# Block-sparse attention with a max-out feed-forward: global scores of two heads over two tiles at once, keys and queries loaded in row pairs and turned by halves on TensorE

## Chip, cores and metric

One core of one Trainium2 chip. The metric is the device time of one execution in microseconds; lower is better. Engines are named as in the profile: PE is TensorE's matmul stream, PEld its weight loads, DVE is VectorE, ACT is ScalarE, POOL is GpSimd, SP issues most DMAs.

## The reference

Four batches of eight heads, 768 positions of 64 numbers, in blocks of 32 (24 blocks). A query block sees its own block and the two beside it, three sampled blocks, and the first and the last block; the first and the last query block see everything. The result goes through three 512 x 768 matrices, of which the maximum is taken, and a 768 x 512 matrix.

```python
scores = scale * np.matmul(q, k.transpose(0, 1, 3, 2))
mask = np.abs(blk_i - blk_j) <= window
mask = mask | (blk_i == 0) | (blk_j == 0) | (blk_i == n_blocks - 1) | (blk_j == n_blocks - 1)
for qb in range(n_blocks):
    for kb in sampled_blocks[qb]:
        mask[qb * block:(qb + 1) * block, kb * block:(kb + 1) * block] = True
scores = np.where(mask, scores, -1000000000.0)
attn = softmax(scores)            # with 1e-09 added to the sum
x = (attn @ v), heads side by side
h = np.maximum(np.maximum(x @ w1, x @ w2), x @ w3)
return (h @ w_out).astype(np.float32)
```

All inputs are float32. The kernel splits each operand of the large matmuls into a high and a low float16 part and adds three products (`PASSES`: high-high, high-low, low-high).

## The kernel before

**Units.** A batch is twelve units of 64 queries with all eight heads: eleven sparse ones (two query blocks, 256 gathered keys for each) and one global unit "G" (the first and the last query block, all 768 keys). After every fourth unit the feed-forward for their 256 tokens is put on the list: 216 matmuls of 256 columns (L894, 18 groups of 12), then 36 of 512 columns (L920). The order of units in a batch is G, 10, 8, 9, then 0 to 3, then 4 to 7.

**Keys and queries.** `load_k` brings a batch's keys into three stage tiles, two DMAs for each (one for the even rows, one for the odd ones), so that a run in HBM is one row of one head, 256 bytes. Queries come the same way into `qn`, in pieces of up to 128 rows for twice 128 partitions. `turn_k` (L566) and `prep_q` (L643) turn them on PE: one turn is four transposes of 128 x 128 float32 into one PSUM bank, each for two heads side by side; ACT writes the scaled high part (L574, L647) and DVE the low part (L577, L650) into `kt` and `qt`. A batch has six turns of keys; each of the twelve query tiles (three in each batch) has two turns. Turns, and the transposes of a finished unit (L867), share one PSUM bank (`tp_ps`), and, while an operation's priority is below `Plan(4)`'s 4, the two banks of the second score tile as well.

**Attention.** `gather` copies sampled key blocks into `kg` (L685; a register that holds the block's number is loaded first, L351, on the engine that copies) and fetches rows of values from HBM with an indirect DMA on POOL (L699). `sparse_item` makes the scores of four heads (L775), the maximum (L749), the exponents (L784), and `probs` splits them (ACT L727, POOL L728) and turns them by a DMA transpose on SP (L732); for the first units (`TURNED`) PE turns them instead (L720). `values` multiplies by the values (L799). The global unit does four items, one for each `i` and `hd`: scores (L818) of two heads `u` at the same `hd`, over the two key tiles `a`, both in one score tile of two banks; maximum over both (L746), two exponents (L828), values (L840). `hd` picks partitions 0 to 63 or 64 to 127 of `qt` and `kt`, `u` the output rows 0 to 63 or 64 to 127. `finish_unit` divides (L858 to L860), turns (L867) and stores the high and low part for the feed-forward.

**Weights.** `prep_weights` loads 24 pieces (8 groups `g` of three), casts each (L437 on POOL or L440 on ACT, whichever the planner finds sooner free), puts it together on DVE (L444), scales it by a sum of squares on PE (L388, L376), and writes a high part (ACT L466) and a low part (DVE L475). The first feed-forward needs the first six groups, its second matrix the last two.

**The order.** `Plan` is a list of operations with an engine, an assumed duration, keys read and written, and a priority. `Plan.order` runs through them once at build time, and the instructions are emitted in that order, so every engine works through a fixed list. Where the plan sees PE without work for more than 0.2 us, `gaps` and `idle` fill the hole with matmuls whose result is never used (fillers, L991), one for each 0.11 us. A filler is a real instruction: it takes its time whether or not the hole is there.

## Time and profile before

| | |
|---|---|
| median of 3 runs | 678.12 us (677.71 to 678.25) |
| profiled execution | 669.58 us, its span 667.8 us |
| mean granted clock | 0.992 |
| busy DVE, ACT, POOL | 57%, 57%, 47% of the span |
| DMA | 110.45 MB, mean 165 GB/s; 162,993 of 199,065 packets under 512 bytes |

The profiled execution is faster than the median of the runs by 8.5 us; stages and durations are read from it, and differences are put on the median. A busy PE says little by itself here, since the fillers count as busy. The rows that matter are therefore shown by stage: from the start to the first scores, to the first feed-forward matmul, to the second feed-forward, and the rest.

### The profile page before, as it was taken

What the parts mean: (1) busy time and instruction counts of PE and PEld (TensorE: products, weight loads), DVE (VectorE), ACT (ScalarE), POOL (GpSimd) and SP (SyncE); (2) the same over time, 40 slices, a digit from 0 to 9 for tenths busy, and PEclk for the clock granted to TensorE, in tenths of its full rate; (3) what the DMA queues carried; (4) which work ended last, traced back from release to release, by engine and by line L of the source; (5) the groups of instructions that cost most, each with busy time, mean ns of one, the idle gap of its engine ahead of it and who ended that gap; (6) DMA issues with size and microseconds to landing.
All of it is one profiled execution on the core that took longest, in us unless ns stands there. A gap on an engine that the chain in (4) does not pass through costs nothing.

```text
span 667.8 us, 26558 instructions
## 1 busy us (share of the span) xinstructions
PE 626.4 (94%) x11249; PEld 482.8 (72%) x11249; DVE 382.4 (57%) x1076; ACT 379.8 (57%) x789; POOL 314.1 (47%) x405
## 2 busy tenths in 40 slices
PE   8797997999999998989999988999999989999997
PEld 7675876886886875777867865777868857758684
DVE  1598786886754666653754863355746765543120
ACT  0366664668745867766538764386548764463111
POOL 1333567353553667645235776255236775462010
PEclk9999999899999999999999999999999999999999
DMA  9599699999865889998486799989575897593000
GB/s 191 173 275 255 145 252 184 218 167 237 212 144 147 112 163 196 216 215 195 115 225 113 131 179 225 220 137 177 149 191 101 165 213 153 119 164 74 33 1 32
DMA packets 199065, 110.45 MB, mean 165 GB/s; under 512 B 162993, under 2 KB 184610, under 8 KB 198946
## 3 DMA queue, kind: packets, MB, share of 16 engines
q1 hardware_dynamic: 189090, 73.61, 57.7%
q0 software_dynamic: 9856, 35.15, 20.9%
q8 instruction: 88, 1.44, 0.9%
q14 instruction: 31, 0.25, 0.1%
HBM read 68.77 MB, written 12.70 MB: 122 GB/s over the span
## 4 chain that ended last, share of the span: by engine, by line
PE 83%; issue 4%; DMA 4%; DVE 4%; ACT 3%; another core or an unknown queue 0%; SPq 0%; DVEq 0%; POOL 0%; ACTq 0%; POOLq 0%
PE f_ps L894 42%; PE f_ps L920 13%; PE av_ps L799 6%; PE s_ps L775 6%; PE f_ps L991 5%; DMA pts<-phl 2%; PE s_ps L818 2%; PE tp_ps L867 2%; PE tp_ps L643 2%; PE av_ps L840 1%; PE tp_ps L566 1%; DMA vscr<-vhl 1%; PE tp_ps L376 1%; PE tp_ps L388 1%; DVE nm L749 1%
## 5 line engine op out<-in xcount | busy, mean ns | idle before, releaser
L894 PE MATMUL f_ps<-xg,w_hl 128*128 128x256 f16 x2592 | 304.4, 275 | 7.3 <-issue 4.2
L894 PEld LDWEIGHTS <-w_hl 128*128 128x128 f16 x2592 | 250.1, 99 | 49.4 <-issue 17.2
L728 POOL TENSOR_TENSOR phl<-pr,phl 128x512 f16<-128x512 f32 (+1 forms) x110 | 126.8, 1155 | 110.2 <-ACT phl L727 74.0
L902 DVE SCALAR_TENSOR_TENSOR hf<-f_ps,hf 128x256 f32<-128x256 f32 x144 | 60.8, 422 | 94.6 <-PE f_ps L894 86.3
L906 POOL TENSOR_TENSOR ht<-hf,ht 128x256 f16<-128x256 f32 x72 | 51.4, 714 | 124.0 <-ACT ht L905 123.9
L699 POOL DMA_INDIRECT vg<-vscr,rows_of x88 | 83.4, 948 | 48.8 <-PE av_ps L799 19.2
L784 ACT ACTIVATE pr<-s_ps,nm,qsm 128x256 f32<-128x256 f32 x176 | 92.5, 562 | 18.9 <-DVE nm L754 17.1
L920 PE MATMUL f_ps<-wo_hl,ht 128*128 128x512 f16 x432 | 99.7, 379 | 1.5 <-issue 1.5
L749 DVE TENSOR_REDUCE nm<-s_ps 128x2 f32<-128x512 f32 x88 | 60.4, 686 | 40.5 <-PE s_ps L775 28.4
L920 PEld LDWEIGHTS <-ht 128*128 128x128 f16 x432 | 40.5, 98 | 48.0 <-issue 5.7
L991 PE MATMUL f_ps<-ident 128*128 128x256 f16 x561 | 71.6, 277 | 1.5 <-DVE ident L268 1.5
L727 ACT CAST phl<-pr 128x512 f16<-128x512 f32 (+1 forms) x110 | 65.2, 594 | 2.2 <-DMA pts<-phl 0.3
L905 ACT CAST ht<-hf 128x256 f16<-128x256 f32 x72 | 29.0, 403 | 63.7 <-DVE hf L902 62.4
L991 PEld LDWEIGHTS <-ident 128*128 128x128 f16 x561 | 53.8, 100 | 10.4 <-issue 2.3
L799 PEld LDWEIGHTS <-pts 128*32 128x32 f16 x4224 | 39.5, 95 | 22.7 <-issue 19.6
L799 PE MATMUL av_ps<-vg,pts 128*32 128x65 f16 (+1 forms) x4224 | 47.4, 196 | 8.8 <-issue 6.2
L685 POOL COPY kg<-kt 128x256 f16 x88 | 37.6, 450 | 34.9 <-PE s_ps L775 29.7
L898 ACT ACTIVATE hf<-f_ps 128x256 f32<-128x256 f32 x72 | 27.5, 382 | 41.8 <-PE f_ps L894 39.0
L775 PE MATMUL s_ps<-kg,qt 64*32 64x256 f16 x2112 | 45.7, 272 | 5.8 <-issue 3.1
L685 ACT COPY kg<-kt 128x256 f16 x88 | 31.6, 402 | 26.1 <-PE s_ps L775 21.2
L775 PEld LDWEIGHTS <-qt 64*32 64x32 f16 x2112 | 24.1, 91 | 15.8 <-issue 12.3
L754 DVE TENSOR_SCALAR nm<-nm,qsm 128x1 f32<-128x1 f32 x192 | 32.5, 207 | 2.3
(150 smaller groups left out, 636.0 us busy)
## 6 DMA issues: line engine op xcount, KB each, us to landing
stage<-in_moe_w_dram SPq DMA_DIRECT2D x14, 511.0 KB
vscr<-vhl SPq DMA_DIRECT2D x12, 520.0 KB
stage<-in_k_dram SPq DMA_DIRECT2D x24, 256.0 KB
stage<-in_v_dram SPq DMA_DIRECT2D x12, 512.0 KB
qn<-in_q_dram SPq DMA_DIRECT2D x20, 256.0 KB
out_dram<-ob SPq DMA_DIRECT2D x20, 256.0 KB
stage<-in_moe_w_out_dram SPq DMA_DIRECT2D x5, 511.8 KB
vg<-vscr SPq DMA_DIRECT2D x16, 130.0 KB
```

Source lines behind the costliest of these rows:

```text
L685: (A.copy if by == 2 else eng.tensor_copy)(out=dst, in_=src)
L699: plan.add("POOL", 1.02, lambda c=c: L.indirect_dma_start(out=vgj[: 6 * HB, c].rearrange("p e h x -> p (e h x)"), out_offset=None, in_=vsc ...
L727: plan.add("ACT", 0.05 + 0.565 * n / 512, lambda: A.copy(out=hl[:, :n], in_=prt[:, :n]), r=PRK(it), w=[hk], pri=pri, alts=[("DVE", 0.6 * n ...
L728: plan.add("POOL", 1.2 * n / 512, lambda: L.tensor_tensor(out=hl[:, n : 2 * n], in0=prt[:, :n], in1=hl[:, :n], op=ALU.subtract), r=PRK(it) ...
L749: plan.add("DVE", 0.7, lambda: V.tensor_reduce(out=n[:, 0:2], in_=both()[:, :, :256], axis=AX.X, op=ALU.max), w=[ks, (ks, 0), (ks, 1)], pr ...
L775: T.matmul(out=s_ps[r * BS : (r + 1) * BS, hd * 512 : hd * 512 + 256], lhsT=q_t[hp, tq, 2 * i + u, q0 + c * BS : q0 + (c + 1) * BS], rhs=k ...
L784: plan.add("ACT", 0.56, lambda hd=hd: A.activation(out=prt[:, hd * 256 : hd * 256 + 256], in_=s_of(job)[:, hd * 512 : hd * 512 + 256], fun ...
L799: T.matmul(out=av_ps[r * BS : (r + 1) * BS, 2 * i + hd, :w], lhsT=pv[:, tp, hd, e, r * BS : (r + 1) * BS], rhs=vgj[:, c, e, h, (D + 2) * t ...
L894: T.matmul(out=pf, lhsT=w_hl[f][:, j, g, wp], rhs=x[:, g, xp, :], start=g == 0 and n == 0, stop=g == G - 1 and n == 2)
L902: plan.add("DVE", 0.42, lambda h=h, pf=pf: V.scalar_tensor_tensor(out=h, in0=pf, scalar=2.0 ** -14, in1=h, op0=ALU.mult, op1=ALU.max), r=[ ...
L920: T.matmul(out=f2_ps, lhsT=hts[:, f, hp, t * P : (t + 1) * P], rhs=wo_hl[f // 3][:, f % 3, wp], start=f == 0 and n == 0, stop=f == NF - 1 ...
L991: T.matmul(out=f_ps[fb][:, :256], lhsT=x[:, :P], rhs=x, start=True, stop=True)
```

## The change

Three things, and numbers of the plan.

1. **Loads.** Keys are loaded as values are (`load_v(k, ...)`): one DMA for a stage tile, a partition holding two neighbouring rows of each head, 512 bytes in one run. Queries come into `qn[P, H, 2, D]` the same way, one DMA for 256 rows, or two (224 and 32 rows) in the group that ends the sequence.
2. **Turns.** Since a head's 64 columns for one parity `e` are no longer beside the next head's, a turn is eight matmuls with the identity as the moving operand, each with 64 weight columns (one head), into the upper or lower half of the PSUM rows. They are plain float32 matmuls where there were transposes.
3. **Global scores.** `global_items` takes both `hd` for one `i`: for each key tile `a` a score tile whose two banks are the two heads `hd`, with `hd` as the innermost loop. Each of the two tiles has its own maximum (two columns); a third DVE operation joins them, then come two bias operations and the four exponents. Both score tiles are held until their exponents are done.

The numbers: `TURNED` 2 to 3 (unit 2 is turned on PE too), `POOL_LOW` with 2 in it (the low part of the third piece of each weight group is made by two POOL operations, L471 and L472, in place of one on DVE), all 24 casts of weights on POOL, sampled copies of slot 0 on ACT in place of DVE for the first units (with their register loads), `Plan(8)` for 4 (three turning banks for longer), `WSL` 0.5 for 0.8 (weights earlier), earlier loads of the next batch, and priorities.

```diff
-PV, TURNED, POOL_LOW = -1, 2, ()
-TP, HOLD, WPRI, WSL = 0.45, 3.0, 2.0, 0.8
+PV, TURNED, POOL_LOW = 0.2, 3, (2,)
+TP, HOLD, WPRI, WSL = 0.45, 3.0, 2.0, 0.5
...
-    qn = sbuf([P, 2, H, D], F32, "qn")
+    qn = sbuf([P, H, 2, D], F32, "qn")
...
-    plan = Plan(4)
+    plan = Plan(8)
...
-            ), 0)] if 1 else ())
+            ), 0)] if 0 else ())
...
-        sts = k_sts[b] = load_k(b, pri, after)
+        sts = k_sts[b] = load_v(k, b, pri, after)
...
-            src = stage[sts[a]].rearrange("p (e g x) -> p e g x", e=2, g=G)
+            src = stage[sts[a]].rearrange("p (h e d) -> p e h d", h=H, e=2)
...
                     for y in range(4):
                         g, e = 2 * half + y // 2, y % 2
-                        T.transpose(tv[:, y], src[:, e, g], ident)
+                        for hd in range(2):
+                            T.matmul(out=tv[hd * D : (hd + 1) * D, y], lhsT=src[:, e, 2 * g + hd], rhs=ident, start=True, stop=True)
...
-        for p0, w, r in pieces(n):
-            p0, e = p0 % P, p0 // P
-            plan.add("SP", 0.45, lambda p0=p0, e=e, w=w, r=r: Y.dma_start(out=qn[p0 : p0 + w, e], in_=src[r : r + w]),
-                     r=after, w=[("qn", e, p0 > 0)], pri=pri, land=2.2, move=1.8 * w / P)
+        for p0, w, r in [(0, whole, r0)] + ([(whole, 2 * P - whole, 0)] if whole < 2 * P else []):
+            plan.add("SP", 0.45, lambda p0=p0, w=w, r=r: Y.dma_start(
+                out=qn[p0 // 2 : (p0 + w) // 2].rearrange("p h e d -> p h (e d)"),
+                in_=q[b, :, r : r + w, :].rearrange("h (p e) d -> p h (e d)", e=2)),
+                r=after, w=[("qn", p0 > 0)], pri=pri, land=2.2, move=2.05 * w / 256)
...
-                for g in range(G):
-                    T.transpose(tv()[:, g], qn[:, e, 2 * g : 2 * g + 2], ident)
-            hi, lo = (to[:, t, :, e * P : (e + 1) * P] for t in range(2))
+                for h in range(H):
+                    T.matmul(out=tv()[h % 2 * D : (h % 2 + 1) * D, h // 2], lhsT=qn[:, h, e], rhs=ident, start=True, stop=True)
+            hi, lo = (to[:, t].rearrange("p g (x e) -> p g x e", e=2)[:, :, :, e] for t in range(2))
...
-                by = (0,1,2)[t] if pri < 8 else t
+                by = (2,1,2)[t] if pri < 8 else t
...
+    def global_items(U, b, i, q_c, pri):
...
+        for a, job in enumerate(jobs):
+            def scores(a=a, job=job):
+                for x, (tq, tk) in enumerate(PASSES):
                     for u in range(2):
+                        for hd in range(2):
+                            hp = slice(hd * 64, hd * 64 + 64)
+                            T.matmul(
+                                out=s_of(job)[u * 64 : u * 64 + 64, hd * 512 : hd * 512 + 384],
+                                lhsT=q_t[hp, tq, 2 * i + u, 192:256],
+                                rhs=kt[hp, :, tk, 2 * i + u, a],
+                                start=x == 0, stop=x == 2,
+                            )
...
+            plan.add("DVE", 0.95, lambda na=na, job=job: V.tensor_reduce(
+                out=na[:, 0:2], in_=s_of(job).rearrange("p (d x) -> p d x", d=2)[:, :, :384], axis=AX.X, op=ALU.max),
...
-        pri -= 0
+        pri -= 2
...
-        by = (0,1,2)[t] if 8 > 0 else t
+        by = (2,1,2)[t] if 8 > 0 else t
...
-        if x == max(gx, 6 if U < 12 else 6) and b + 1 < B:
-            prep_v(b + 1, U + 3, [("unit", U)])
-        if x == (6 if U < 12 else 4) and b + 1 < B:
+        if x == max(gx, 4 if U < 12 else 5) and b + 1 < B:
+            prep_v(b + 1, U + 7, [("unit", U)])
+        if x == (4 if U < 12 else 3) and b + 1 < B:
...
-            prep_q(nx // 12, nx % 12 // 4, nx - 2.0, [("unit", 0)] if U == 1 else ())
+            prep_q(nx // 12, nx % 12 // 4, nx - 3.0, [("unit", 0)] if U == 1 else ())
```

In the program fillers fall from 561 to 464. Before the first scores there are 153 and then 122, from there to the first feed-forward matmul 314 and then 322, after it 94 and then 20.

On PE, just after the sums of squares of the first keys (`stage_78` and `stage_79` are the first two key tiles, L566 and L643 turn keys and queries, L991 are fillers), before:

```order
L376 MATMUL tp_ps<-qsm_99,ones 128x1
L566 MATMUL s_ps_141<-ident,stage_78 128x8x16 x4
L566 MATMUL s_ps_141<-ident,stage_79 128x8x16 x4
L643 MATMUL tp_ps<-ident,qn 128x128 x4
L991 LDWEIGHTS ident
L991 MATMUL f_ps_143<-ident 128x256
```

and now, L556 and L635 being the turns, L1000 the fillers:

```order
L376 MATMUL tp_ps<-qsm_99,ones 128x1
L556 MATMUL s_ps_141<-ident,stage_78 64x8x16 x8
L556 MATMUL s_ps_141<-ident,stage_79 64x8x16 x8
L1000 LDWEIGHTS ident
L1000 MATMUL f_ps_143<-ident 128x256
L635 MATMUL tp_ps<-ident,qn 64x128 x8
```

A turn is now eight instructions with 64 output rows each. Between the first query turn and the second stand 36 fillers (there were 7), and ahead of each of the three sums of squares of keys 14 (there were 28).

On ACT, at the end of the register loads with which its list begins, before:

```order
L351 TENSOR_LOAD samp
L351 ISA x2
L574 ACTIVATE kt_89<-s_ps_141,ksm_103 128x8x64 x2
L647 ACTIVATE qt_97<-tp_ps,qsm_99 128x4x128
L647 ACTIVATE qt_97<-s_ps_141,qsm_99 128x4x128
L574 ACTIVATE kt_89<-s_ps_141,ksm_103 128x8x64
L574 ACTIVATE kt_89<-tp_ps,ksm_103 128x8x64
L440 CAST ob_134<-xg_128 128x512
```

and now:

```order
L351 TENSOR_LOAD samp
L351 ISA x2
L639 ACTIVATE qt_97<-tp_ps,qsm_99 128x512
L564 ACTIVATE kt_89<-s_ps_141,ksm_103 128x8x64 x2
L639 ACTIVATE qt_97<-tp_ps,qsm_99 128x512
L564 ACTIVATE kt_89<-s_ps_141,ksm_103 128x8x64 x2
L564 ACTIVATE kt_89<-tp_ps,ksm_103 128x8x64
L564 ACTIVATE kt_89<-s_ps_141,ksm_103 128x8x64
```

There are 28 such loads ahead of the first high part where there were 14, and the casts of weights are gone from between the high parts.

On POOL, in the stretch where the first weights are split (`kt_90` holds the weights on their way, `vg` the gathered values, `kg` the sampled keys), before:

```order
L685 ISA
L685 COPY kg_93<-kt_89 128x256
L728 TENSOR_TENSOR phl_117<-pr_113,phl_117 128x512
L437 CAST ob_134<-xg_129 128x512
L728 TENSOR_TENSOR phl_118<-pr_114,phl_118 128x512
L699 DMA vg_94<-vscr_136,rows_of 96x2080 x2
```

and now:

```order
L437 CAST ob_135<-stage_83 128x512
L471 TENSOR_SCALAR kt_90<-kt_90,w_s 128x512
L472 TENSOR_TENSOR w_hl_63<-kt_90,w_hl_63 128x4x128
L691 DMA vg_94<-vscr_136,rows_of 96x2080 x2
L437 CAST ob_134<-xg_129 128x512
L471 TENSOR_SCALAR kt_90<-kt_90,w_s 128x512
L472 TENSOR_TENSOR w_hl_64<-kt_90,w_hl_64 128x4x128
L677 ISA
L677 COPY kg_93<-kt_89 128x256
```

A gather (L691) and the copies of sampled keys now stand behind two-step low parts of weights, eight of which are on POOL altogether.

129 lines of the change are left out of this document (61 added, 68 removed).

## The prediction, made before the changed kernel had run

> **What bounds the kernel now.** I read the page's busy shares first, then four stages by windows, then the fillers in the same windows, then PE's timeline. The page's first line, and the four stages, with the busy time of PE, PEld, DVE, ACT and POOL in each, then the clock, and the share and rate of DMA:
>
> ```profile
> PE 626.4 (94%) x11249; PEld 482.8 (72%) x11249; DVE 382.4 (57%) x1076; ACT 379.8 (57%) x789; POOL 314.1 (47%) x405
> 0.00:34.78 34.78, 28.24 (x255) 23.83 (x255) 11.87 (x44) 9.15 (x14) 9.87 (x39) 1.00 0.80 187
> 34.78:100.60 65.82, 59.83 (x1141) 48.67 (x1141) 54.56 (x138) 44.71 (x87) 30.49 (x36) 1.00 0.90 231
> 100.60:164.87 64.27, 58.82 (x1068) 46.79 (x1067) 48.30 (x129) 40.66 (x83) 32.67 (x35) 0.95 1.04 204
> 164.87:663.20 498.33, 479.49 (x8790) 363.55 (x8789) 267.69 (x767) 284.61 (x608) 241.05 (x297) 1.00 0.76 151
> ```
>
> and the fillers alone (PE, PEld), for the same windows:
>
> ```profile
> 0.00:34.78 34.78, 20.73 (x153) 15.36 (x153) 1.00 0.80 187
> 34.78:100.60 65.82, 38.66 (x315) 29.52 (x314) 1.00 0.90 231
> 100.60:164.87 64.27, 11.04 (x88) 8.16 (x86) 0.95 1.04 204
> 164.87:663.20 498.33, 1.20 (x8) 0.78 (x8) 1.00 0.76 151
> ```
>
> Ninety-four per cent says little. In the last stage PE is busy 479.5 of 498.3 us with next to no fillers, and no other engine above 285: there every us of PE work counts in full. In the first two stages 59 us of PE are fillers; what decides are the chains over DMA, ACT and DVE which those fillers cover. The third, from the first feed-forward matmul to the second feed-forward, lies between.
>
> **Stage 1, the loads.** The rate of DMA in forty slices of 0.75 us of the first 30 us, PE's rows there, and one from POOL's and one from ACT's list:
>
> ```profile
> GB/s 0 0 7 133 287 229 202 203 218 218 218 218 216 218 218 213 212 313 325 284 254 53 45 42 130 340 349 307 335 358 207 53 14 0 0 82 266 373 386 322
> 6.10 0.39 PE L388 MATMUL tp_ps<-qn 128*128 128x128 bf16 x4 [0.59 <-DMA qn<-in_q_dram]
> 9.38 0.62 PE L388 MATMUL s_ps<-stage 128*128 128x128 bf16 x8
> 9.85 3.22 PE L991 MATMUL f_ps<-ident 128*128 128x256 f16 x28
> 36.25 5.41 PE L991 MATMUL f_ps<-ident 128*128 128x256 f16 x48
> 10.44 0.99 POOL L483 MEMSET ob<- 128x512 int32 x2 [7.73 <-issue]
> 20.54 1.26 ACT L574 ACTIVATE kt<-s_ps,ksm 128x512 f16<-128x512 f32 x2 [18.32 <-PE s_ps L566]
> ```
>
> Queries and keys (2 MB in 256-byte runs) flow at about 218 GB/s; the values behind them (512-byte runs) at about 313. In 512-byte runs the 2 MB take 2.0 / 313 = 6.4 us for 9.2. Forty-eight fillers take 5.41 and 28 take 3.22, so one is 0.11 us; 31 fewer are 3.4 us, and the first row shows a wait for queries that shorter loads cut. But ACT gets in the way: POOL's fourteen register loads took the 7.73 us of that gap (2.71 to 10.44), 0.55 us each, so ACT's 28 end near 2.7 + 15.4 = 18.1 us. Before, its first high part came at 20.54. So the stage gains at least 20.54 - 18.1 = 2.4 us, and, if PE also loses fewer waits (by its window it was not busy for 6.5 us of the stage), up to 5. I take 3.5, with dearer turns (below) in it.
>
> **The turns.** Two turns in the third stage and what follows each:
>
> ```profile
> 138.59 0.60 PE L643 MATMUL tp_ps<-ident,qn 128*128 128x128 f32 x4
> 139.03 1.15 PE L894 MATMUL f_ps<-xg,w_hl 128*128 128x256 f16 x9
> 17.42 0.73 PE L376 MATMUL s_ps<-ksm,ones 128*128 128x1 f32 x6
> 45.84 0.82 PE L840 MATMUL av_ps<-vhl,pts 128*64 128x65 f16 x36
> L840 PE MATMUL av_ps<-vhl,pts 128*64 128x65 f16 (+1 forms) x576 | 11.7, 196 | 0.8 <-issue 0.8
> ```
>
> A turn takes PE from 138.59 to 139.03, 0.44 us, 0.110 for each of four transposes. What a plain float32 matmul costs is seen in one place only: three instructions of the program (L376) stand as six records, so each is done in two. A new turn is therefore sixteen records of 128 moving columns. Their price is bounded. From below by bfloat16 records of 128 columns (L388, eight from 9.38 to 9.85, 0.059 each), two at a time in the two halves of the columns: 16 x 0.059 / 2 = 0.47 us. From above by float32 records like the transposes, one at a time: 16 x 0.110 = 1.76. For two at a time speaks L840, which also alternates 64-column halves: 36 in 0.82, of which one matmul's own 0.196 is tail, so 0.018 each, where 65 columns of L388's price would be 0.030. The nearest row in type and in columns is the transpose, the nearest in shape of tile L840; I take 0.110, halved: 0.88 us, or 0.44 more for each turn.
>
> The Trainium skill, FP8 and Floating Point Precision (TensorE Precision Notes), speaks against the change: true float32 goes through the array in four passes; the two records of L376 fit that if each makes two. By that rule alone, at one bfloat16 pass of 0.059 us, eight matmuls would take 1.89 us a turn, and the sum below would end near 719 us in place of 674. TensorEngine Tiling (Key Properties) says that different tiles load weights and multiply in parallel, which would halve it to 0.94 (677 us); L840's row agrees in kind, but no run here shows it for float32.
>
> How many turns count is in the same windows, for L566 and then L643 in the last stage, four records to a turn:
>
> ```profile
> 164.87:663.20 498.33, 10.85 (x72) 8.51 (x72) 1.00 0.76 151
> 164.87:663.20 498.33, 11.25 (x72) 8.19 (x72) 1.00 0.76 151
> ```
>
> Eighteen and eighteen; four more lie in stages 2 and 3, eight in stage 1. So +36 x 0.44 = 15.8 us in stage 4 and 0.9 each in stages 2 and 3.
>
> **The global scores.**
>
> ```profile
> 34.79 1.52 PE L818 MATMUL s_ps<-kt,qt 64*64 64x384 f16 x24
> 42.24 1.16 PE L818 MATMUL s_ps<-kt,qt 64*64 64x384 f16 x12
> 43.34 0.72 PE L991 MATMUL f_ps<-ident 128*128 128x256 f16 x5
> 60.32 0.85 PE L775 MATMUL s_ps<-kg,qt 64*32 64x256 f16 x48
> 61.10 0.72 PE L991 MATMUL f_ps<-ident 128*128 128x256 f16 x5
> ```
>
> Twelve matmuls of one head take 1.10 us (0.092 each), but where two heads stand one behind the other 24 take 1.46, from 34.79 to the fillers at 36.25 (0.061): their halves of the rows overlap where they meet. Alternating all along is what L775 does over eight tiles, 48 in 0.78; with 384 for 256 columns and four tiles for eight that is 0.049 each. I take 0.049 (bounds 0.061 and the 0.040 of perfect sharing): twelve groups of twelve in stage 4 save 12 x 12 x 0.043 = 6.2 us (4.5 to 7.5), the first batch 1.3. The maximum and its bias grow by one small DVE operation for each pair, beside feed-forward matmuls. The pair's two score tiles are now held together, so the next sparse scores wait until the last exponents; feed-forward matmuls lie behind them on PE and cover it at 1 to 2 us for each of three batches. I charge nothing. Nor for queries written to every second element, the earlier loads of the next batch and the priorities: DVE and ACT, which carry them, are busy 268 and 285 of stage 4's 498 us. Were a write of a query half to take twice its time there, PE would meet it only where a turn's bank is wanted at once.
>
> **Stages 2 and 3.** Eight more fillers in stage 2 (+0.9) against the 1.3 saved and 0.9 for turns: +0.5. In stage 3, PE waits in these rows:
>
> ```profile
> 113.47 0.56 PE L799 MATMUL av_ps<-vg,pts 128*32 128x65 f16 x48 [2.54 <-DMA pts<-phl]
> 147.15 3.65 PE L991 MATMUL f_ps<-ident 128*128 128x256 f16 x32
> 151.50 0.85 PE L775 MATMUL s_ps<-kg,qt 64*32 64x256 f16 x48 [0.69 <-ACT wo_hl L466]
> ```
>
> The 32 fillers and the wait behind them cover the last weights, which `WSL` 0.5 brings earlier; 74 fewer fillers after the first feed-forward matmul are 8.1 us. Of 3.2 us of waits in these rows and of the clock of 0.95 over 64 us (another 3.2) I count half as gone, 3.2. With 0.9 for turns stage 3 gives -10.4. What the plan's earlier weights lean on is POOL:
>
> ```profile
> L728 POOL TENSOR_TENSOR phl<-pr,phl 128x512 f16<-128x512 f32 x15 | 21.1, 1407 | 27.5 <-ACT phl L727 18.8 <-issue 5.4 <-DMA qn<-in_q_dram 3.2
> L437 POOL CAST ob<-stage 128x512 f16<-128x512 bf16 x7 | 6.5, 951 | 1.6 <-DVE kt L444 1.6
> ```
>
> (from 34.78 to 164.87 us). Thirteen more casts (24, where POOL had 11) at 0.95 are 12.4, and eight low parts at two operations of L728's 1.41 are 22.5. POOL goes from 63.2 of 130.1 us to 98: three quarters full, in a fixed order, with gathers behind. DVE and ACT are relieved of the same operations.
>
> **The sum.** -3.5 + 0.5 - 10.4 + (15.8 - 6.2) = -3.8 us against the span of 667.8 us, which would become 664.0. Put on the median of 678.1: 674.3 us.
>
> **The rivals.**
>
> *Halves that do not overlap.* If the float32 halves go one at a time, a turn is 1.76 us: 40 turns at 0.88 more, 35.2, and 3.5 in stage 1 give 678.1 - 3.8 + 38.7 = 713.0 us, slower. The place is PE in stage 4. Without the 17.6 us for 40 turns the sum is -21.4, so the change loses from a turn of 0.44 + 21.4 / 40 = 0.98 us on. For it: every float32 record in the trace is a full-width one. Against: L840.
>
> *Cheap turns.* If a record costs no more than a bfloat16 one and halves overlap, a turn stays near 0.47: -3.8 - 16.4 - 1.6 (stage 1) = -21.8 gives 656.3 us. For it: nothing in the trace shows what 128 moving columns cost in such a record. Against: the transposes, of the same type, take 0.110.
>
> *POOL late.* The low parts stand ahead of gathers, so values wait, or the first feed-forward waits for weights. Eight at 2.8 us are 22.5; with half of it on PE's path, where fillers have been taken away, 678.1 - 3.8 + 11.2 = 685.5 us. For it: three quarters full, in a fixed order. Against: L728's row above has 27.5 us of POOL's idle time, and most of it is a wait for ACT, not room that is missing.
>
> **How the numbers follow.** Forecast 0.44, halves that do not overlap 0.18, cheap turns 0.22, POOL late 0.16. The forecast's own range, from the bounds on the scores, stage 1 and half of the waits, is 667 to 681. 0.2% (1.4 us) is about what a measurement tells here. Faster: 0.31 of the forecast's 0.44, cheap turns 0.22, 0.02 of POOL late: 0.55. Within: 0.07 and 0.02, 0.09. Slower: 0.06, 0.18 and 0.12, 0.36. The range runs from 650 (below cheap turns) to 700, which takes in halves that overlap in part and leaves out most of the first rival.
>
> **What would show it.** Sixteen records to a turn, and 0.88 us from a turn's start to the next operation's; 0.59 us for twelve global matmuls; the first scores near 31 us; ACT's first high part near 18; no filler block ahead of the second feed-forward matrix; waits of L799 or L894 on POOL if POOL is late. I am wrong in the main if a turn takes over 1 us, or if PE in stage 4 waits for something that this trace does not show waiting.

## The result, and the profile after

The changed kernel is slower: 703.09 us median of four runs (696.72 to 710.57) against 677.91 us, a ratio of 1.0363 with a 95% interval of 1.0286 to 1.0441. On another chip, beside the experiments below, the same kernel took 703.47 us against 670.02 us there: 1.0549 (1.0452 to 1.0646). The kernel before differs more between chips than the changed one does, so what follows compares ratios, or runs of one chip.

Medians are over all runs of a kernel, ratios leave out runs in a slower state of the chip, and the changed kernel's first profiled execution (710.57 us) was such a run. It is used for the order of things, for durations of single instructions and for the first three stages, whose ends the profile of the other chip (e5, 696.6 us span) has within 0.7 us; the last stage is read from e5.

The page's first line of the changed kernel, and the four stages by windows, with the columns of the prediction (PE, PEld, DVE, ACT, POOL busy, clock, share and rate of DMA):

```profile
PE 649.7 (92%) x11736; PEld 496.4 (70%) x11736; DVE 387.1 (55%) x1062; ACT 380.2 (54%) x792; POOL 341.1 (48%) x432
0.00:35.86 35.86, 29.45 (x320) 24.01 (x321) 13.53 (x44) 7.81 (x13) 11.95 (x42) 1.00 0.65 172
35.86:107.92 72.06, 66.31 (x1277) 53.28 (x1277) 55.30 (x139) 47.96 (x98) 42.32 (x46) 1.00 0.91 228
107.92:164.99 57.07, 52.99 (x1003) 41.63 (x1003) 45.57 (x111) 38.04 (x78) 45.64 (x49) 1.00 0.97 207
```

Its fillers in the second and third of these windows:

```profile
35.86:107.92 72.06, 40.22 (x323) 30.27 (x322) 1.00 0.91 228
107.92:164.99 57.07, 2.52 (x20) 1.87 (x20) 1.00 0.97 207
```

The second feed-forward starts at 164.99 us (165.55 on the other chip) where it started at 164.87: none of the 13.4 us that the forecast saw there has arrived. The rest of the loss lies behind it. The last stage of the kernel before up to the end of its span, and of the changed kernel on the other chip:

```profile
164.88:667.80 502.92, 479.48 (x8790) 363.54 (x8789) 267.68 (x767) 285.28 (x609) 241.05 (x297) 1.00 0.75 150
165.55:696.60 531.05, 490.79 (x9142) 373.38 (x9139) 283.63 (x770) 285.33 (x606) 240.14 (x298) 0.98 0.75 142
```

The stage is 28.1 us longer. PE's busy time grew by 11.3 us, close to the 9.6 that the forecast had for the whole stage. The other 16.8 us are time in which PE does nothing: 40.3 us for 23.4. What PE waited for in that stage, line by line, in total, times and longest, first before and then changed:

```profile
PE f_ps L894 <- issue: 4.2, 7, 2.2
PE s_ps L775 <- issue: 3.1, 5, 1.4
PE av_ps L799 <- issue: 3.1, 4, 1.6
...
PE f_ps L920 <- issue: 1.5, 2, 1.3
```

```profile
PE av_ps L791 <- issue: 9.2, 4, 4.4
PE s_ps L767 <- issue: 8.5, 4, 4.2
PE av_ps L847 <- DMA pts<-phl: 5.4, 2, 2.9
PE f_ps L901 <- issue: 2.9, 3, 1.4
PE tp_ps L635 <- issue: 2.7, 1, 2.7
```

"Issue" is time in which the profile names nothing that PE waited for: 11.9 us before, 23.3 us now. Turned probabilities that land late (`pts<-phl`) add 5.4 ahead of the global unit's values (L847), where the kernel before had no such row in this stage. Eighteen stalls of "issue", none over 2.2 us, became twelve of up to 4.4; in the first profile of the changed kernel the same stage has 26.7 us in 25 stalls, so the sum repeats and the places do not.

One of them, from PE's timeline of the changed kernel on the other chip (e5); then the windows ahead of it, in it and behind it; then the rate of DMA in forty slices of the stall and what the queues moved in it (packets, MB, time of their packets as a share of 16 engines):

```profile
286.11 0.52 PE L791 MATMUL av_ps<-vg,pts 128*32 128x65 f16 x44
291.00 0.25 PE L791 MATMUL av_ps<-vg,pts 128*32 128x65 f16 x4 [4.37 <-issue]
```

```profile
282.60:286.63 4.03, 4.03 (x146) 3.05 (x145) 2.71 (x5) 3.12 (x7) 1.96 (x3) 1.00 1.08 257
286.63:291.00 4.37, 0.00 (x2) 0.00 (x0) 0.61 (x2) 0.09 (x1) 0.33 (x1) 1.00 1.37 105
291.00:295.00 4.00, 4.00 (x53) 2.94 (x53) 2.09 (x7) 1.77 (x4) 1.84 (x2) 0.58 0.81 131
```

```profile
GB/s 284 52 21 16 19 19 96 279 434 269 317 253 134 2 0 0 0 2 7 7 9 9 9 9 14 218 272 230 7 7 9 7 7 9 7 30 284 288 293 258
q1 hardware_dynamic: 1726, 0.43, 132.5%
q14 instruction: 1, 0.01, 2.6%
q8 instruction: 1, 0.02, 1.5%
```

PE stops inside a group of value matmuls, after 44 of 48 that all read the same tiles, so no operand is missing. DVE, ACT and POOL do next to nothing in the same 4.4 us. On the DMA engines packets stand open all the time (share 1.37), yet in half of the slices they move 0 to 20 GB/s, and one packet of program arrives on each of two queues. The profile counts these two queues ("instruction") on the same 16 DMA engines as the data. That PE waits in such a place for its next piece of program, held up there, is what the rows fit; no run tried it alone. What a stall costs besides its own length is in the third window: the granted clock is 0.58 over the next 4 us, which is 1.7 us more. (The Trainium skill, TensorE: Matmul & The Clock Gate, section on the HAM clock gate, says that PE gets half the pulses after a quiet stretch until about 3.4 us of work have passed; the row agrees.)

The turns and the global scores, from PE's timeline in the first profile of the changed kernel:

```profile
6.70 3.08 PE L1000 MATMUL f_ps<-ident 128*128 128x256 f16 x14
...
18.70 1.09 PE L635 MATMUL tp_ps<-ident,qn 128*64 128x128 f32 x16
19.72 4.11 PE L1000 MATMUL f_ps<-ident 128*128 128x256 f16 x36
23.76 1.09 PE L635 MATMUL tp_ps<-ident,qn 128*64 128x128 f32 x16
24.78 0.39 PE L1000 MATMUL f_ps<-ident 128*128 128x256 f16 x2
...
42.09 0.68 PE L812 MATMUL s_ps<-kt,qt 64*64 64x384 f16 x12
42.70 0.61 PE L1000 MATMUL f_ps<-ident 128*128 128x256 f16 x4
```

A turn holds PE from 18.70 to 19.72 and from 23.76 to 24.78, 1.02 us; twelve global matmuls hold it for 0.61.

### The profile page after: what moved, and what is told of

Its sections match the earlier page's. It is cut to its first block, busy times and chain, and to the rows that moved or that the text cites. A ratio compares the mean times of both kernels' runs of the same rounds, so it can differ in the third digit from the quotient of the medians.

```text
span 708.8 us, 27535 instructions
## 1 busy us (share of the span) xinstructions
PE 649.7 (92%) x11736; PEld 496.4 (70%) x11736; DVE 387.1 (55%) x1062; ACT 380.2 (54%) x792; POOL 341.1 (48%) x432
## 4 chain that ended last, share of the span: by engine, by line
PE 72%; DMA 8%; issue 7%; DVE 5%; ACT 3%; POOL 3%; SPq 1%; DVEq 0%; ACTq 0%; POOLq 0%
PE f_ps L901 34%; PE f_ps L927 11%; DMA pts<-phl 6%; PE av_ps L791 5%; PE f_ps L1000 5%; PE s_ps L767 5%; PE tp_ps L635 3%; PE tp_ps L556 2%; DMA stage<-in_k_dram 2%; PE tp_ps L874 1%; PE s_ps L556 1%; PE s_ps L812 1%; POOL ob L437 1%; PE av_ps L847 1%; POOL kt L471 1%
## 5 line engine op out<-in xcount | busy, mean ns | idle before, releaser
L901 PE MATMUL f_ps<-xg,w_hl 128*128 128x256 f16 x2592 | 309.3, 278 | 8.0 <-issue 6.0
L901 PEld LDWEIGHTS <-w_hl 128*128 128x128 f16 x2592 | 252.7, 100 | 55.0 <-issue 19.5
L720 POOL TENSOR_TENSOR phl<-pr,phl 128x512 f16<-128x512 f32 (+1 forms) x108 | 122.4, 1138 | 109.2 <-ACT phl L719 63.3
L691 POOL DMA_INDIRECT vg<-vscr,rows_of x88 | 82.9, 942 | 55.0 <-PE av_ps L791 34.5
L1000 PE MATMUL f_ps<-ident 128*128 128x256 f16 x464 | 60.4, 278 | 4.0 <-DVE ident L268 2.4
L767 PE MATMUL s_ps<-kg,qt 64*32 64x256 f16 x2112 | 49.8, 285 | 13.4 <-issue 9.7
L791 PEld LDWEIGHTS <-pts 128*32 128x32 f16 x4224 | 39.8, 95 | 23.3 <-issue 23.0
L677 ACT COPY kg<-kt 128x256 f16 x104 | 38.1, 405 | 27.9 <-PE s_ps L767 16.1
L1000 PEld LDWEIGHTS <-ident 128*128 128x128 f16 x464 | 44.1, 100 | 12.5 <-issue 4.9
L677 POOL COPY kg<-kt 128x256 f16 x88 | 35.5, 424 | 23.2 <-PE s_ps L767 22.0
L767 PEld LDWEIGHTS <-qt 64*32 64x32 f16 x2112 | 26.1, 94 | 26.8 <-issue 21.8
L905 ACT ACTIVATE hf<-f_ps 128x256 f32<-128x256 f32 x72 | 27.4, 381 | 28.8 <-PE f_ps L901 27.3
L639 ACT ACTIVATE qt<-tp_ps,qsm 128x512 f16<-128x512 f32 x21 | 17.6, 837 | 39.6 <-PE tp_ps L635 38.2
```

The costliest lines, as they stand in the source:

```text
L677: (A.copy if by == 2 else eng.tensor_copy)(out=dst, in_=src)
L691: plan.add("POOL", 1.02, lambda c=c: L.indirect_dma_start(out=vgj[: 6 * HB, c].rearrange("p e h x -> p (e h x)"), out_offset=None, in_=vsc ...
L720: plan.add("POOL", 1.2 * n / 512, lambda: L.tensor_tensor(out=hl[:, n : 2 * n], in0=prt[:, :n], in1=hl[:, :n], op=ALU.subtract), r=PRK(it) ...
L767: T.matmul(out=s_ps[r * BS : (r + 1) * BS, hd * 512 : hd * 512 + 256], lhsT=q_t[hp, tq, 2 * i + u, q0 + c * BS : q0 + (c + 1) * BS], rhs=k ...
L791: T.matmul(out=av_ps[r * BS : (r + 1) * BS, 2 * i + hd, :w], lhsT=pv[:, tp, hd, e, r * BS : (r + 1) * BS], rhs=vgj[:, c, e, h, (D + 2) * t ...
L901: T.matmul(out=pf, lhsT=w_hl[f][:, j, g, wp], rhs=x[:, g, xp, :], start=g == 0 and n == 0, stop=g == G - 1 and n == 2)
```

## Experiments

Ratios are to the kernel before, run beside each kernel on the same chip; the interval is 95%. The three parts of the change are called numbers, loads and turns, and global scores.

| run | what it is | median us | before beside it | ratio |
|---|---|---|---|---|
| e1 | before + loads and turns | 714.29 | 667.48 | 1.0682 (1.0597 to 1.0767) |
| e2 | before + global scores | 678.73 | 667.48 | 1.0176 (1.0115 to 1.0237) |
| e3 | before + numbers | 673.55 | 667.48 | 1.0054 (1.0011 to 1.0096) |
| e4 | changed, old loads and turns | 685.44 | 667.48 | 1.0257 (1.0192 to 1.0323) |
| e5 | changed, again | 703.47 | 670.02 | 1.0549 (1.0452 to 1.0646) |
| e6 | changed, true price of a turn in the plan | 718.20 | 670.02 | 1.0754 (1.0634 to 1.0874) |
| e7 | before + turns by halves | 686.95 | 670.02 | 1.0289 (1.0194 to 1.0383) |
| e8 | before + full-width matmuls as turns | 689.94 | 670.02 | 1.0350 (1.0250 to 1.0450) |
| e9 | e7 + keys by pairs | 705.15 | 674.69 | 1.0392 (1.0300 to 1.0484) |
| e10 | e7 + queries by pairs | 710.59 | 674.69 | 1.0551 (1.0474 to 1.0627) |
| e11 | e2 without its late fillers | 687.41 | 674.69 | 1.0167 (1.0104 to 1.0229) |
| e12 | changed, old global scores | 718.87 | 674.69 | 1.0630 (1.0548 to 1.0711) |
| e13 | e1's loads in e7's order | 706.78 | 675.04 | 1.0553 (1.0401 to 1.0705) |
| e14 | e10's loads in e7's order | 702.13 | 675.04 | 1.0447 (1.0302 to 1.0593) |
| e15 | e7's loads in e10's order | 712.29 | 675.04 | 1.0601 (1.0466 to 1.0736) |
| e16 | e7 again | 697.50 | 675.60 | 1.0346 (1.0309 to 1.0383) |
| e17 | e1 again | 719.17 | 675.60 | 1.0663 (1.0615 to 1.0712) |
| e18 | e7's loads in e1's order | 713.81 | 675.60 | 1.0571 (1.0510 to 1.0631) |

### The parts by themselves (e1 to e4, e12)

**Loads and turns alone**, put on the kernel before:

```diff
-                        T.transpose(tv[:, y], src[:, e, g], ident)
+                        for hd in range(2):
+                            T.matmul(out=tv[hd * D : (hd + 1) * D, y], lhsT=src[:, e, 2 * g + hd], rhs=ident, start=True, stop=True)
...
-        sts = k_sts[b] = load_k(b, pri, after)
+        sts = k_sts[b] = load_v(k, b, pri, after)
```

> The kernel before with the pair loads and the half turns alone; its own plan numbers and global scores. Theory A (the turns are PE work that nothing covers): the changed kernel's profile has 1.0 us for a turn where there were 0.44, so 40 turns outside the start cost 40 x 0.55 = 22 us and the loads give back 2 to 3: 697 us. Theory B (the new plan numbers cost the time, the turns are covered by waits that PE had anyway): within 5 us of before, 675 to 683 us. Theory C (PE is held up by its own instruction stream, seen as idle time put down to issue, and more records make it worse): like A, but with issue waits of over 20 us after the start, where before had 12.

47 us, twice what the turns' price gives. By the two profiles PE is busy 33.4 us longer and idle 13.4 us longer. "Issue" is 25.6 us over the span where the kernel before has 17.7, so theory C's stalls are at most 8 of the 47.

**Global scores alone:**

```diff
-                for hd in range(2):
-                    global_item(U, b, i, hd, q_c, pri)
+                global_items(U, b, i, q_c, pri)
```

> The kernel before with the global scores of two heads over two tiles alone. All theories: 192 matmuls at 0.05 in place of 0.09 us save 8 us of PE work, 6 of them in the stage without fillers: 670 to 673 us. If both score tiles held together stop the sparse scores behind them, 678 us or more, with waits of PE on ACT's exponents or on the DMA transposes after each global unit.

Its 192 global matmuls went from 17.8 to 9.6 us of PE as wanted, and the kernel still lost 11 us: the fillers of the program rose from 561 to 724. Both score tiles are held until their exponents are done, the plan sees PE without work and fills it. The 163 additional fillers keep PE busy for 19.8 us; less the 8.2 us saved that is 11.6, about the loss.

**Numbers alone:**

```diff
-PV, TURNED, POOL_LOW = -1, 2, ()
-TP, HOLD, WPRI, WSL = 0.45, 3.0, 2.0, 0.8
+PV, TURNED, POOL_LOW = 0.2, 3, (2,)
+TP, HOLD, WPRI, WSL = 0.45, 3.0, 2.0, 0.5
...
-    plan = Plan(4)
+    plan = Plan(8)
```

> The kernel before with the plan numbers alone (weights earlier, POOL's low parts and casts, sampled copies on ACT, three turning banks for longer, next batch earlier, priorities); old loads, turns and global scores. Theory A: fewer fillers and waits before the second feed-forward, 665 to 672 us. Theory B: the new order is what costs, 690 us or more, with the issue waits of the changed kernel (27 us after the start). Theory C: like before unless small matmuls now stand closer together.

Nearly nothing, 0.5% slower: neither theory A's gain nor theory B's loss.

**The changed kernel with old loads and turns**, that is numbers and global scores:

```diff
-        sts = k_sts[b] = load_v(k, b, pri, after)
+        sts = k_sts[b] = load_k(b, pri, after)
```

> The changed kernel with the loads and turns of before: new plan numbers and global scores. Theory A: 703 less 22 to 26, and the start a little later: 677 to 683, or below before if the numbers help as forecast (660 to 668). Theory B: still slower than before, 690 to 700 us. Theory C: issue waits fall back to about 12 us when the additional records go.

2.0 points above numbers alone on the same chip: global scores cost as much here as on the kernel before. Theory C fell: without the additional records "issue" is 33.5 us over the span, more than the 27.4 of the changed kernel.

**The changed kernel with the old global scores**, that is numbers, loads and turns:

```diff
-                global_items(U, b, i, q_c, pri)
+                for hd in range(2):
+                    global_item(U, b, i, hd, q_c, pri)
```

> The changed kernel with the old global scores: numbers, loads and turns alone. The changed kernel stands at 1.055 on one chip and 1.036 on another, numbers alone at 1.005, loads and turns alone at 1.068. If the parts add, the global scores of the changed kernel gain or cost what they do alone (1.018): 1.04 here. If they gain their 8 us because the changed plan sees few holes (22 fillers after the first feed-forward matmul), 1.065 here. If the numbers make the loads harmless, below 1.04.

As much as loads and turns alone. The parts do not add: 0.5, 6.8 and 1.8% are more than the whole change costs (3.6 and 5.5% on two chips).

### What a turn costs (e7, e8, e16)

**Turns by halves, with the old loads:**

```diff
-                        T.transpose(tv[:, y], src[:, e, g], ident)
+                        for hd in range(2):
+                            T.matmul(out=tv[hd * D : (hd + 1) * D, y], lhsT=src[:, e, g, hd * D : (hd + 1) * D], rhs=ident, start=True, stop=True)
```

> The kernel before with its own loads, only the turns made by eight plain float32 matmuls of 64 columns each in place of four transposes. Theory A: 48 turns x 0.55 us = 26 us more than before in all, of which stage 1 hides little: ratio 1.035 to 1.045. Theory L (the pair loads and the queries written to every second element are what costs, as loads and turns together cost 47 us on the kernel before): ratio 1.02 or less. Theory S (PE's stalls come with the number of instructions): 1.05 or more, as with the loads.

**Plain matmuls of full width, no halves:**

```diff
-                        T.transpose(tv[:, y], src[:, e, g], ident)
+                        T.matmul(out=tv[:, y], lhsT=src[:, e, g], rhs=ident, start=True, stop=True)
```

> The kernel before with its own loads, each turn as four plain float32 matmuls of 128 columns against the identity in place of four transposes: eight records in place of four, and no halves. If the two halves of the columns overlap fully, this takes as long as the turns by halves (about 1.0 us a turn, within 3 us of that kernel), and the price is that of plain float32 against a transpose. If halves overlap only in part, it is cheaper than they are: by 0.1 us a turn, 5 us in all. If a record of a plain matmul is dearer than a transpose's (above 0.110 us), a turn is above 0.9 us here.

A query turn and what follows it, on PE's timeline of the kernel with halves, and of the one with full width:

```profile
21.14 1.04 PE L644 MATMUL tp_ps<-ident,qn 128*64 128x128 f32 x16
22.11 0.94 PE L992 MATMUL f_ps<-ident 128*128 128x256 f16 x7
```

```profile
21.51 1.06 PE L643 MATMUL tp_ps<-ident,qn 128*128 128x128 f32 x8
22.40 0.93 PE L991 MATMUL f_ps<-ident 128*128 128x256 f16 x7
```

0.97 us by halves, 0.89 by full width, 0.44 by transposes. Eight full-width records take 8 x 0.111, the price of a transpose each; sixteen half-width ones take 0.061 each. So halves overlap nearly in full, and the price is that of a plain float32 matmul, two records where a transpose has one. In time the two kernels cannot be told apart (1.029 and 1.035). The turns alone are worth 17 us on one chip and 22 on the next, below, between theory L's bound and the lower edge of theory A's range:

> Turns by halves alone once more (old loads, old order), on the chip of the next two runs: 1.029 before. If the ratio is above 1.04 here, the differences that were put down to loads and order are differences of chips.

1.0346: below the 1.04 named there, so the turns cost much the same on two chips.

### The plan told the price (e5, e6)

> The changed kernel once more, on the chip of the next three runs, so that they can be set against it. On record its ratio to the kernel before is 1.0363 [1.0286, 1.0441]; the version with old loads and turns (N and G only) had 1.0257 on another chip, though the profiled spans of the two differ by 25 us. Theory A (the turns cost their price, 48 x 0.55 = 26 us, on PE's path) expects 1.04 to 1.06 here; theory D (loads and turns are nearly free beside the new numbers) expects 1.036 or less.

1.0549, in theory A's range; the first chip's 1.0363 was at theory D's edge. One kernel's ratio can differ by 2 points between chips.

```diff
-                plan.add("PE", TP, turn, r=SK(sts[a]) + ["ident", ("k", "s", b)], free=[hk, lk],
+                plan.add("PE", 1.0, turn, r=SK(sts[a]) + ["ident", ("k", "s", b)], free=[hk, lk],
```

(and the same for queries)

> The changed kernel with the plan told that a turn takes 1.0 us in place of 0.45; nothing else. Theory P (part of the loss is the plan's: it is told half the price, so its order sets operations and fillers for turns that end too early) expects 5 to 15 us less than the changed kernel beside it. Theory A (the price itself is paid wherever it is put) expects within 3 us of it.

Both theories missed. With the true duration the plan's order is 15 us worse than with half of it on the same chip; PE's idle time put down to "issue" rose from 27.4 to 47.7 us over the span. An order that comes from truer numbers can be 2% worse on the chip.

### Held score tiles (e11)

```diff
-            if i in gaps:
+            if i in gaps and at < 165:
                 idle(*gaps[i])
```

This leaves out 128 fillers of the kernel with global scores alone, whose result nothing uses.

> The kernel before with the global scores of two heads over two tiles, and the fillers after the plan's 165 us left out: 128 fillers, which compute nothing that is used. Theory A' (the two held score tiles make holes in the plan only; filled, they cost 128 x 0.11 to 0.125 = 14 to 16 us of PE time, and unfilled FFN work closes them): 14 us below the 1.0176 that the same kernel had with them, a ratio of 0.99 to 1.00. Theory H (the holes are real, because the next scores wait for the held tiles): PE waits there instead, ratio 1.01 to 1.02.

The last stage with the fillers, their own share of it, and the last stage without them:

```profile
163.11:671.50 508.39, 484.34 (x8916) 375.16 (x8908) 273.00 (x772) 287.33 (x608) 239.89 (x297) 0.99 0.80 149
163.11:671.50 508.39, 15.98 (x128) 12.19 (x128) 0.99 0.80 149
```

```profile
170.94:687.10 516.16, 481.78 (x8788) 366.72 (x8780) 269.96 (x772) 286.24 (x608) 240.48 (x297) 0.97 0.79 147
```

By the ratio theory H held: 16 us of fillers gone, and nothing won. PE is idle for 34.4 us instead of 24.0, and its other work takes 481.8 us instead of 484.3 - 16.0 = 468.4. But the waits are not for the held tiles, where theory H put them. Without the fillers the waits of that stage with a named releaser add up to 13.5 us, against 1.6 with them; among them are

```profile
PE f_ps L909 <- DVE xg L887: 2.5, 3, 0.9
PE tp_ps L882 <- DVE qt L650: 2.2, 3, 1.7
...
PE f_ps L909 <- ACT xg L886: 1.4, 3, 0.5
```

`xg` holds the rows of a unit just finished, on which the next feed-forward waits, and at each of three global units the first pair's scores stand just ahead of it. DVE and PE there:

```profile
215.20 1.81 DVE L829 TENSOR_REDUCE nm<-s_ps 128x2 f32<-128x768 f32 x2
216.93 0.41 DVE L887 TENSOR_TENSOR xg<-tp_ps,xg 128x256 f16<-128x256 f32 x1
217.40 5.29 PE L909 MATMUL f_ps<-xg,w_hl 128*128 128x256 f16 x47 [0.78 <-DVE xg L887]
```

DVE makes both maxima (1.81 us) before the low part of those rows. In the kernel before it made one there (0.96 us), and PE had the scores of the next item to do meanwhile, from 209.47 to 210.56; now the first pair holds both score tiles. With fillers, 17 of them stand in this place (206.95 to 208.81); without them PE waits for `xg` for 1.2 to 1.4 us. So these holes are real for the most part, and a held tile costs by the work that it keeps away. This is read from the rows: with the scores the order of the list changes too, and no run holds it fixed.

The clock of the two profiled runs in that stage, 0.99 and 0.97, may explain most of the 13.4 us by which the other work is longer. It is no clear property of the kernels: over the runs behind the two ratios the mean clock is 0.974 to 0.984 with the fillers and 0.972 to 0.982 without. Whether fillers pay for themselves by the clock stays open. (The two come from different chips; the ratios, 1.0176 and 1.0167, from runs beside the kernel before on each.)

### Loads or order (e9, e10, e13 to e15, e17, e18)

Turns and loads together cost 6.8%, turns 2.9%. First the two loads apart, each with the turns by halves.

```diff
-        sts = k_sts[b] = load_k(b, pri, after)
+        sts = k_sts[b] = load_v(k, b, pri, after)
```

> The kernel before with turns by halves, and the keys alone loaded by pairs of rows (one DMA of 512 KB for two of 256 KB); queries loaded as before. Turns by halves alone gave a ratio of 1.029, with pair loads of keys and queries 1.068: some 26 us hang on the loads. Theory K (the one large key load stands ahead of the transposes of probabilities, the gathers and PE's own program pieces in the DMA engines): 1.055 to 1.07, with 10 us more idle time of PE than turns alone. Theory Q (it is the queries): 1.03. Theory O (no transfer matters, the plan's order comes out another and worse one with any change of a load's numbers): both this and the queries alone land anywhere between 1.03 and 1.07, and their extras do not add up to 0.039.

```diff
-    qn = sbuf([P, 2, H, D], F32, "qn")
+    qn = sbuf([P, H, 2, D], F32, "qn")
...
+        for p0, w, r in [(0, whole, r0)] + ([(whole, 2 * P - whole, 0)] if whole < 2 * P else []):
```

> The kernel before with turns by halves, and the queries alone loaded by pairs of rows (one DMA of 512 KB, written out to every second element of a row after the turn); keys loaded as before. Theory Q (the first wait for queries is longer, a group of queries must be there whole, strided writes take ACT and DVE longer): 1.05 to 1.07. Theory K: 1.03. Theory O: see the keys.

1.0 and 2.6 points on top of 2.9: together they nearly make up the 6.8 (the ratios come from three chips), and theory Q is nearest. But each also gives the plan another list of loads, and so another order. The next runs take loads and order apart: new loads, in pieces that stand on the list as the old ones did,

```diff
+                plan.add("SP", 0.45, lambda i=i, a=a, e=e: Y.dma_start(
+                    out=stage[i][64 * e : 64 * e + 64].rearrange("p (h x) -> p h x", h=H),
+                    in_=k[b, :, a * 256 + 128 * e : a * 256 + 128 * e + 128, :].rearrange("h (p e) d -> p h (e d)", e=2),
+                ), r=after, w=SK(i)[e : e + 1], pri=pri, land=2.2, move=1.8)
```

> Keys and queries by pairs of rows and turns by halves, as in the kernel before with loads and turns (ratio 1.068), but each pair load split into two DMAs of half the rows, which stand on the plan's list with the old numbers: PE and POOL run through the very order of the kernel with turns by halves alone (1.029). Theory O (the loads themselves are harmless or a gain; the plan, told of other loads, comes to a worse order): 1.02 to 1.035. Theory X (the transfers, the writes to every second element or contention cost it): 1.055 to 1.07.

for the queries alone,

```diff
+        for p0, w, r in pieces(n):
+            plan.add("SP", 0.45, lambda p0=p0, w=w, r=r: Y.dma_start(
+                out=qn[p0 // 2 : (p0 + w) // 2].rearrange("p h e d -> p h (e d)"),
```

> The same for the queries alone (keys loaded as before): PE in the order of turns by halves alone. Theory O: 1.02 to 1.035. Theory X: 1.05, as the queries by pairs had (1.055).

and old loads under the new list, two DMAs in one operation of the plan, first for the queries,

```diff
+                while x < p0 + w:
+                    y = min(p0 + w, (x // P + 1) * P)
+                    Y.dma_start(out=qn[x % P : x % P + y - x, x // P], in_=src[r + x - p0 : r + y - p0])
+                    x = y
```

> The other way about: queries loaded in the old way (runs of 256 bytes, no strided writes), with the plan told of one load for 256 rows, so that PE runs through the very order of the kernel with queries by pairs (1.055). Theory O: 1.05 to 1.06. Theory X: 1.03.

then for keys and queries, with the two other corners beside it on one chip:

```diff
+            def load(i=i, a=a):
+                for e in range(2):
+                    Y.dma_start(
```

> Loads and turns on the kernel before once more (new loads, new order): 1.068 before. By theory O and theory X alike 1.06 to 1.075.

> Old loads of keys and queries and turns by halves, in the order of PE that the kernel with loads and turns has: the last corner of the square of loads and order. New loads in the old order had 1.055. If the order costs what it did with queries alone (1.029 to 1.060), this is at 1.055 to 1.065, and loads and order each cost some 2.5% that do not add up in full. If only the loads cost, 1.03.

On that chip: old loads in the old order 697.50 us, old loads in the new order 713.81, new loads in the new order 719.17. By the ratios the order alone is 2.2 points, some 15 us; the new loads then add 0.9 points, some 6 us, whose intervals (1.0510 to 1.0631 and 1.0615 to 1.0712) barely overlap. New loads in the old order (e13) were at 1.0553 on another chip, 2.1 to 2.6 points above turns by halves. So either step by itself costs about 2 points, the two together 3.2, as the last expectation had it: they do not add up in full. For the queries alone, old loads in the new order (e15, 1.0601) and new loads in the old order (e14, 1.0447) both lie above turns by halves (1.029 and 1.035 on other chips), with intervals that are 3 points wide and overlap. Theories O and X were both right in part; which weighs more is not settled. The third and fourth stage of the old order, and of the new one, with the old loads in both:

```profile
103.58:164.23 60.65, 58.34 (x1092) 45.87 (x1091) 51.39 (x132) 41.67 (x84) 31.74 (x35) 1.00 0.95 210
164.23:690.80 526.57, 502.28 (x9222) 377.09 (x9221) 269.86 (x767) 287.05 (x609) 241.12 (x297) 0.99 0.73 144
```

```profile
104.97:176.56 71.59, 68.44 (x1287) 54.72 (x1285) 59.66 (x156) 49.99 (x97) 35.79 (x40) 1.00 1.02 206
176.56:709.60 533.04, 504.43 (x9134) 379.73 (x9132) 263.16 (x752) 283.05 (x601) 236.16 (x294) 0.98 0.73 141
```

The new order has 195 more PE instructions ahead of the second feed-forward in its third stage, 68 of them fillers, and the last stage, with 88 instructions less to do, takes 6.5 us longer. Over the span PE is busy 10.2 us longer (664.4 for 654.2) with four fillers less, at a mean clock of 0.982 for 0.993 (0.976 to 0.982 and 0.985 to 0.993 over the runs behind the ratios), and idle 8.6 us longer, of which "issue" is 1.7 (21.5 for 19.8). Which move in the order does that stays open.

No version that was tried beats the kernel before.

## Why the prediction was wrong, point by point

**The sign was wrong**: 674.3 us was forecast, 703.1 measured, 3 us above the range. Up to the second feed-forward 13.4 us of gain are missing; the rest of the 28.8 is the last stage, 28.1 us longer for 9.6 by the profile of the other chip (18.5 us, 3 more than the medians leave).

**Price of a turn: mis-sized.** "I take 0.110, halved: 0.88 us" became 0.97 to 1.02. Sixteen records and overlapping halves were right; e8 shows that the record's price, 0.11 at full width, was right as well, and that a half-width record costs 0.061 to 0.064 and not 0.055. That puts a turn at the 0.98 us from which, by the prediction's own working, the change loses: with 0.55 for 0.44 more a turn, 40 turns cost 4.4 us more than forecast. The rule of the Trainium skill that the prediction set beside this (FP8 and Floating Point Precision, TensorE Precision Notes: four passes for float32; TensorEngine Tiling, Key Properties: tiles in parallel) gave 0.94, nearer than the row that was taken; e8's 0.22 us for a plain matmul is 3.8 times the 0.059 of a bfloat16 pass.

**Number of turns in the last stage: too many.** By windows, the changed kernel's key turns (L556), sixteen records to a turn, and its query turns (L635) in the last stage:

```profile
107.92:164.99 57.07, 6.12 (x96) 1.00 0.97 207
164.99:708.80 543.81, 14.01 (x192) 0.97 0.73 139
164.99:708.80 543.81, 20.63 (x288) 0.97 0.73 139
```

Twelve and eighteen, not thirty-six in all: six key turns, 6.1 us, now stand ahead of the second feed-forward, since the next batch's keys are loaded earlier. The prediction charged them to stage 4, and did not see that stage 3 would have to carry them.

**Global scores: right in size, wrong in price.** 0.61 us for twelve (0.59 forecast), and 7.9 us less PE time in all (7.5 forecast). The step that failed is "I charge nothing" for the two held score tiles, since feed-forward matmuls "cover it": e2 loses 1.8% with the cheaper scores in it, as the plan fills 19.8 us more, and e11 shows holes that are real in part: the feed-forward that was to cover them waits itself, behind the two maxima on DVE. That is some 19 us of difference, 11 lost where 8 were to be won, on the kernel before, and 2.0 points again between e3 and e4. In the changed kernel as a whole it costs less: without it (e12) the ratio is 1.063, no better than with it. That fits the case in e12's expectation in which the plan sees few holes (2 fillers in the last stage, for 128 in e2); it is not shown.

**Stage 1: the gain didn't come.** First scores at 35.86 us, not near 31. The loads are faster, 290 GB/s for 218, as the rate of DMA in slices of 0.75 us shows:

```profile
GB/s 0 0 12 116 301 284 213 289 293 289 290 290 292 291 289 291 289 289 294 294 298 330 325 128 288 305 37 11 0 0 0 0 0 22 0 0 45 267 341 120
```

But they were not what the stage waited for. The working took ACT's register loads for the gate; ACT's first high part came at 19.84, and its row names PE as the releaser:

```profile
19.84 0.83 ACT L639 ACTIVATE qt<-tp_ps,qsm 128x512 f16<-128x512 f32 x1 [17.62 <-PE tp_ps L635]
```

PE came to the turn only at 18.70. Ahead of it PE had waited 2.87 us for the queries, which now come in two loads (448 and 64 KB) and not three, and the first fourteen fillers behind that wait took 3.08 us (the row at 6.70 above), twice the 0.11 each that I used; the granted clock stands as 1.00 there, so why they were slow is open. Behind the turn stand 36 fillers which the plan had put there: they took 4.0 us, until 23.76, and nothing lets a filler be skipped when the hole isn't there. The bank that the second turn writes was read for the last time until 21.49 (DVE, L642), so some 2.3 of the 4.0 us covered nothing.

**Stages 2 and 3: fillers fell, work took their place.** In stage 3 they fell from 88 to 20 as forecast, and the stage from 64.3 to 57.1 us. But stage 2 grew by 6.2 us where 0.5 was forecast. In both together PE's busy time rose from 118.7 to 119.3 us: 7.0 us of fillers went, and 7.6 us of work came, six key turns (6.1 us) and the dearer query turns among it. "Half of the waits" was paid out in part only: PE's idle time in the two stages is 9.8 us for 11.4, and stage 3's clock is 1.00 for 0.95.

**The last stage, and the loads: what broke the forecast.** Its busy time came out at +11.3 us for +9.6. Its idle time, for which the prediction had no term, came out at +16.8. That case was named ("if PE in stage 4 waits for something that this trace does not show waiting"), but as a way to be wrong and without a price. The step that failed is the one that charges nothing behind stage 1 for the new loads, "the earlier loads of the next batch and the priorities", on the ground that DVE and ACT have room: no step asked what the new list does to PE. On the kernel before, with its old numbers, the new loads and the order that they bring cost 3.2 points, some 21 us, beyond the turns (e16, e17 on one chip), where the prediction had a gain. Numbers and priorities without the loads cost 0.5% (e3). The trace of before did show 11.9 us of "issue" in that stage, the largest kind of wait there, and the working did not ask what moves it. Another order moved it by 20 us over the span between e5 and e6, with 43 fillers fewer; between e16 and e18, some 15 us apart, it hardly moved, and there PE's busy time and other waits grew. So an order can cost idle time, busy time and clock. How much of the changed kernel's own 16.8 us is the order, and how much the transfers, no run separates.

**The rivals.** Halves that do not overlap would end at 713 us, and the result is nearer to that than to the forecast, but its mechanism is refuted by e7 and e8. POOL late is not it either: one wait of 1.5 us on POOL in the last stage. Cheap turns fell with the row above. The case that the runs on the kernel before point to, loads whose order costs PE idle time and clock, was not among them.

## What to carry to other kernels

A kernel whose engines run through a list made by a planner has a cost that no sum of durations contains: nearly the same instructions in another order were some 15 us apart here (e16, e18), and a truer number in the planner made it 15 us worse (e5, e6). So when a change touches the planner's inputs, give the order a term and a range of its own, about 2% here, before adding up the parts. To separate the two, keep the old list and swap only the bodies of its operations, as e13 to e15 and e18 do. And a cover ("feed-forward lies behind it") is to be priced by the case that it isn't there, above all where the tile that is held longer is one of two.

## What the runs showed of the hardware

A plain float32 matmul of 128 columns takes 0.22 us, a float32 transpose 0.11: two records for one. Two of 64 columns in the two halves of the array overlap to within 10 to 15% (0.061 to 0.064 us a record for 0.0555).

PE can stop for 4 us in the middle of a group of independent matmuls, with the other engines nearly idle, while DMA packets stand open and hardly anything moves (a share of 1.37, under 20 GB/s in half of the stall). PE's idle time put down to "issue" over the span ranged from 17.7 us (before) to 47.7 (e6), though the first of the two program queues moved 88 packets before and 92 in the changed kernel and 91 in e6: the amount of program hardly differs.

Idle time can be paid twice: 4.37 us of stall were followed by 4 us at a clock of 0.58. And leaving out 128 late fillers, 16 us of PE time, won nothing that the runs can tell (ratios 1.0176 with, 1.0167 without).
